# One weight step of the first MLP spread over two slots, on one core: bits in one, the two parts in the next

## The chip, the cores and the metric

The kernel runs on one core of a Trainium2 chip. The metric is device time in microseconds (us) of one execution; the medians below are over three runs. The core has five engines that work side by side and wait for each other through semaphores: TensorE (PE in the profile; its weight loads are the row PEld), VectorE (DVE), ScalarE (ACT), GpSimd (POOL) and SyncE (SP), the last two of which issue most transfers here.

## The reference

An attention with two kinds of masks over 4 sequences, and two MLPs behind it, all in float32 values; the weights come as float64.

```python
x = attention(q, k, v)                 # 8 heads, 576 positions, head size 64: (2304, 512)
h = x @ w_in                           # MLP 1, d_ff = 2048
g = h * clip(h + 3, 0, 6) / 6
x = g @ w_out
h = x @ w_in2                          # MLP 2
x = (max(h, 0) + log1p(exp(-abs(h)))) @ w_out2
```

Half of the heads see the last 32 positions ("local"), the other half every 32nd position ("strided").

## The kernel before, in words

Every float32 product is made of three products of a shorter type (fp32r): a value is split into its rounded part `hi` and the difference `lo`, and hi·hi, hi·lo and lo·hi are summed in PSUM. A weight needs more, since it comes as float64 words. `w_scale` (ACT, L132) scales its upper words, `w_bits` (DVE, L137 and L140) cuts the lower words and joins both to one float32 tile (`wir`, `wor`). After this, a split makes the two parts: `win_split` of a tile of w_in is a cast on ACT (`wih`, L160) and a difference on DVE (`wil`, L146, through the helper `less`); `wout_split` of a tile of w_out is the same with `woh` (L177) and `wol` (L146). The difference reads what the cast wrote.

MLP 1 runs over five chunks of tokens: chunk 0 has the first 96 positions of all four sequences (384 tokens), chunks 1 to 4 the other 480 of one sequence each. A chunk has 16 steps f, one for each 128 of d_ff. The program walks through `seq`, the 80 pairs (chunk, f), and calls `slot(n, ...)` for each; within a slot every engine keeps the order in which the program writes its instructions (`in_order`). Slot n does on TensorE the 12 matmuls of `pe_h(n)` (h, L774) and then the 12 of `pe_y(n-2)` (L818). Between them stand, for ACT and DVE, `post1` (ACT `r` L787, DVE `r` L788), `post2a` (ACT `gh` L795) and `post2b` (DVE `gl` L801), which make g and its two parts. PSUM has two banks for h, so pe_h(n) waits until DVE's `r` of slot n-2 has read its bank.

Chunk 0 is also the first use of each weight of MLP 1. So its slots carry the weights' work: `w_scale` and `win_bits` of w_in tile f+2, `win_split` of the same tile, and `w_scale`, `wout_bits`, `wout_split` of w_out tile f. `wout_split` also writes the float32 tile to `wdr` in DRAM (L176, issued by POOL), for chunk 1. The 32 loads of 512 KB (w_in L107, w_out L112) are issued by SP into eight buffers; `load_first(k)` issues the k-th of the list `order1`, and each waits until the tile that was in its buffer has been joined.

The attention of the sequence whose tokens come in the next chunk runs in between: `put(s, ...)` places a piece into half-slot s of the table `fill`, and slot n runs the pieces of half-slot 2n between pe_h and pe_y, and those of 2n+1 behind pe_y. For sequence 0 these are the transposes of q and k (`s_trans`), the scores (`a_qk`), mask, maximum, exponent and sum (`a_add`, `a_max`, `a_exp`, `a_sum`, `a_rec`), and the products with v (`a_pt`, `a_pv`, `a_px`), first for the strided heads, then for the local ones.

Of the kernel before, what the change touches and what calls it, by code (L numbers as in the profile page):

```python
# [7 lines left out]
F32 = mybir.dt.float32  # L8
F32R = mybir.dt.float32r
# [13 lines left out]
def attn_two_mlps(  # L23
# [21 lines left out]
    nc = tc.nc  # L45
# [6 lines left out]
    NF = DFF // P  # L52
# [36 lines left out]
    wdr = [dram.tile([P, DM], F32, name=f"wdr{f}") for f in range(NF)]  # L89
# [7 lines left out]
    wst_t, wi_t, wo_t = {}, {}, {}  # L97
# [14 lines left out]
        nc.sync.dma_start(out=t, in_=w_out[l][f * P : (f + 1) * P, :])  # L112
        wst_t[1, l, f] = t

    order1 = [(load_win, 0), (load_win, 1)]
    for f in range(NF):
        order1 += [(load_win, f + 2), (load_wout, f)]

    def load_first(k):
        load, f = order1[k] if k < len(order1) else (None, NF)  # L120
        if f < NF:
            load(0, f, k % 8)
# [6 lines left out]
    def w_scale(o, l, f):  # L129

        h = words(o, l, f, U32)[1].bitcast(F32)
        nc.scalar.activation(out=h, in_=h, func=AF.Prelu, scale=2.0**-112, alpha=-(2.0**32))  # L132

    def w_bits(o, l, f, out=None):
        low, _ = words(o, l, f, U32)
        m, e = words(o, l, f, I32)
        nc.vector.tensor_scalar(  # L137
            out=m, in0=low, scalar1=2.0**-29, scalar2=7.0, op0=ALU.mult, op1=ALU.min
        )
        nc.vector.scalar_tensor_tensor(  # L140
            out=e if out is None else out.bitcast(I32), in0=e, scalar=3, in1=m,
            op0=ALU.logical_shift_left, op1=ALU.bitwise_or,
        )
# [6 lines left out]
    def win_bits(f):  # L150
        wi_t[0, f] = sw_tile("wir", F32)
        w_bits(0, 0, f, wi_t[0, f])
        wst_t.pop((0, 0, f))

    def win_split(f):
        raw = wi_t[0, f]
        hi, lo = (wp.tile([P, KT, P], F32R, tag=f"wi{n}", name=f"wi{n}") for n in "hl")
        wi_t[0, f] = (hi, lo)
        hi, lo = (t.rearrange("p k f -> p (k f)") for t in (hi, lo))
        nc.scalar.copy(hi, raw)  # L160
        less(nc.vector, lo, raw, hi)

    def sw_tile(name, dt=F32R):
        return sw.tile([P, DM], dt, tag="sw", name=name)

    def wout_bits(f):
        wo_t[0, f] = tuple(
            sw_tile(n, dt) for n, dt in (("wor", F32), ("woh", F32R), ("wol", F32R))
        )
        w_bits(1, 0, f, wo_t[0, f][0])  # L170
        wst_t.pop((1, 0, f))

    def wout_split(f):
        raw, hi, lo = wo_t[0, f]
        wo_t[0, f] = hi, lo
        nc.gpsimd.dma_start(out=wdr[f], in_=raw)  # L176
        nc.scalar.copy(hi, raw)  # L177
        less(nc.vector, lo, raw, hi)

# [77 lines left out]
    def prep(k):  # L257

        n, h = divmod(k, 7)
        if k < 0 or n >= 2 * NF2:  # L260
            return
        o, g = divmod(n, NF2)
        if h == 0 and n + 1 < 2 * NF2:
            prep_load(*divmod(n + 1, NF2))
        if h < 2:
            w_scale(o, 1, 2 * g + h)
            w_bits(o, 1, 2 * g + h)
        elif h == 2:
            prep_sums(o, g)
        else:  # L270
            prep_split(o, g, *divmod(h - 3, 2))
# [511 lines left out]
    def post1(l, c, f):  # L783
        n = width(l, c)
        ps = ph_t.pop((l, c, f))[:, :n]
        r = tp.tile([P, SB], F32, tag="g32", name="r", bufs=2)[:, :n]
        nc.scalar.activation(out=r, in_=ps, func=AF.Relu, bias=3.0)  # L787
        mark["DVE"] = nc.vector.scalar_tensor_tensor(  # L788
            out=r, in0=r, scalar=6.0, in1=ps, op0=ALU.min, op1=ALU.mult
        )  # L790
        g32_t[l, c, f] = r

    def post2a(l, c, f):
        hi = gp.tile([P, SB], F32R, tag="gh", name="gh")[:, : width(l, c)]
        mark["ACT"] = nc.scalar.copy(hi, g32_t[l, c, f])  # L795
        g_t[l, c, f] = hi

    def post2b(l, c, f):
        hi = g_t[l, c, f]
        lo = gp.tile([P, SB], F32R, tag="gl", name="gl")[:, : width(l, c)]  # L800
        nc.vector.tensor_tensor(  # L801
            out=lo, in0=g32_t.pop((l, c, f)), in1=hi.bitcast(F32), op=ALU.subtract
        )
        g_t[l, c, f] = (hi, lo)
# [318 lines left out]
    def put(slot, u, *a):  # L1123
        fill.setdefault(max(slot, 0), []).append(lambda: u(*a))

    for b in range(B):
        o = 2 * NF * b
        s0 = o + 2 if b < 2 else o - 1
        for pr in range(NP):
            if b:  # L1130
                put(o - (14 if b > 1 else 5), s_load, b, pr)
                put(o - 5, s_load_v, b, pr)
            put(o + (6 if b < 2 else 3), l_load_qk, b, pr)
            put(o + 18, l_load_v, b, pr)
        if b == 0:
            for n, a in enumerate((("q",), ("k",), ("k", True))):
                put(s0 + n, s_trans, b, *a)
        else:
            for n, a in enumerate((n, pr) for pr in range(NP) for n in "qk"):
                put(s0 + n, s_trans32, b, *a)  # L1140
        for st, qk, pt in ((0, s0 + 4, 13), (1, o + 10, 22)):
            put(qk, a_qk, st, b)
            for e in range(2):
                put(qk + 1, a_add, st, b, e)
                put(qk + 2 + e, a_max, st, b, e)
                put(qk + 3 + e, a_exp, st, b, e)
                put(qk + 4 + e, a_sum, st, b, e)
            put(qk + 6, a_rec, st, b)
            put(o + pt, a_pt, st, b)
            put(o + pt + 3, a_pv, st, b)  # L1150
            put(o + pt + 6, a_px, st, b)

    with ExitStack():
# [5 lines left out]
        for i, t in enumerate(sq0):  # L1159
            nc.sync.dma_start(  # L1160
                out=t.rearrange("p (h i) d -> p h (i d)", h=2),
                in_=qs[:, 2 * i : 2 * i + 2, :II, :].rearrange("p h i d -> p h (i d)"),
# [15 lines left out]
            out=mask, in_=mask, compare_op=ALU.is_ge, fill=NEG / SCALE, base=STRIDE,  # L1178
# [85 lines left out]
        load_first(3)  # L1264
        bmask_make()
        load_first(4)
        for pr in range(NP):
            s_load(0, pr)
        for pr in range(NP):
            s_load_v(0, pr)  # L1270
        for k in range(5, 10):
            load_first(k)
        with after("xh", "xl"):
            win_split(1)

        seq = [(0, c, f) for c in range(NC1) for f in range(NF)]

        def slot(n, l, c, f):
            att = c < B
            first_use = c == 0  # L1280
            last1 = c == NC1 - 1
            k0 = 2 * n - 2 * NF - 14

            if n == NF + 1:
                prep_load(0, 0)
            if last1 and f == 0:
                at.close()
                l2p["x"] = ctx.enter_context(tc.tile_pool(name="l2x", bufs=1, reuse_waits="tile"))
            pe_h(l, c, f)
            if first_use:  # L1290
                if f + 2 < NF:
                    w_scale(0, 0, f + 2)
                    win_bits(f + 2)
            else:
                post1(l, c, f)
                post2a(l, c, f)
            if att:
                for u in fill.get(2 * n, []):
                    u()
            if first_use:  # L1300
                post1(l, c, f)
                post2a(l, c, f)
                if f + 2 < NF:
                    win_split(f + 2)
                w_scale(1, 0, f)
                wout_bits(f)
            post2b(l, c, f)
            prep(k0)
            if n >= 2:
                pe_y(*seq[n - 2])  # L1310
            if att:
                for u in fill.get(2 * n + 1, []):
                    u()
            prep(k0 + 1)
            if first_use:
                wout_split(f)
                load_first(2 * f + 10)
                load_first(2 * f + 11)
            if c == 1:
                split_raw(c, f)  # L1320
            if NF <= n + 3 < 2 * NF:
                load_raw(*seq[n + 3][1:])
            if 2 * NF <= n + 4 < len(seq):
                load_split(*seq[n + 4][1:])
            if last1 and f >= 1:
                kl, r = divmod(f - 1, 7)
                if r == 0 and kl < 2:
                    for o, i in x_load(CHS[0], kl):
                        nc.sync.dma_start(out=o, in_=i)
                elif r == 3:  # L1330
                    x_split(CHS[0], kl, 0)
                    x_sums(CHS[0], kl, False)
                elif r == 4:
                    x_sums(CHS[0], kl, True)
                    x_split(CHS[0], kl, 2)
                elif r == 5:
                    x_split(CHS[0], kl, 1)
# [149 lines left out]
```

## Time and profile before

| | us |
|---|---|
| median of 3 runs | 864.46 (863.44 to 866.81) |
| the profiled execution, its own time | 864.04 |
| its span, first to last instruction | 862.2 |

Busy share of the span: PE 96%, PEld 88%, DVE 74%, ACT 53%, POOL 10%. The mean granted clock of TensorE is 0.988 of full speed. The profile gives, for a stretch of the span, the busy time of each engine (x is the number of instructions), the granted clock and the load of the 16 DMA engines; for an engine, its instructions in order of time, with the time that it sat idle before one and the instruction that released it; and, for pairs of engines, the sum of such waits. A matmul's own duration is longer than the distance to the next one, since they overlap; the distance between two starts tells what one costs.

### The profile page before, as it was taken

What the parts mean: (1) busy time and instruction counts of PE and PEld (TensorE: products, weight loads), DVE (VectorE), ACT (ScalarE), POOL (GpSimd) and SP (SyncE); (2) the same over time, 40 slices, a digit from 0 to 9 for tenths busy, and PEclk for the clock granted to TensorE, in tenths of its full rate; (3) what the DMA queues carried; (4) which work ended last, traced back from release to release, by engine and by line L of the source; (5) the groups of instructions that cost most, each with busy time, mean ns of one, the idle gap of its engine ahead of it and who ended that gap; (6) DMA issues with size and microseconds to landing.
All of it is one profiled execution on the core that took longest, in us unless ns stands there. A gap on an engine that the chain in (4) does not pass through costs nothing.

```text
span 862.2 us, 16753 instructions
## 1 busy us (share of the span) xinstructions
PE 823.7 (96%) x6245; PEld 755.0 (88%) x6245; DVE 637.2 (74%) x1055; ACT 457.3 (53%) x754; POOL 88.4 (10%) x149
## 2 busy tenths in 40 slices
PE   4897899999999999999999999999999999999996
PEld 2796678888878888888888899999999999999995
DVE  5778777676767677866676848788678898587784
ACT  4555554455434445554555457863377844478530
POOL 3000003132311112111211110000000000000000
PEclk8899999999999999999999999999999999999999
DMA  8795888599987999696879599778899787997774
GB/s 244 216 323 163 230 189 303 174 230 350 352 337 227 247 331 318 210 278 212 304 257 319 197 348 298 244 247 249 247 308 343 241 247 224 301 300 242 252 245 110
DMA packets 169504, 225.42 MB, mean 261 GB/s; under 512 B 76432, under 2 KB 91664, under 8 KB 169424
## 3 DMA queue, kind: packets, MB, share of 16 engines
q1 hardware_dynamic: 154304, 176.71, 67.5%
q0 software_dynamic: 13312, 46.67, 14.2%
q10 hardware_dynamic: 1808, 0.98, 0.5%
q8 instruction: 50, 0.82, 0.4%
q14 instruction: 30, 0.25, 0.1%
HBM read 172.88 MB, written 51.38 MB: 260 GB/s over the span
## 4 chain that ended last, share of the span: by engine, by line
PE 54%; issue 16%; DVE 5%; ACT 4%; POOL 3%; DMA 2%; POOLq 0%; SPq 0%; DVEq 0%; ACTq 0%
PE psn L1075 15%; PE psm L931 11%; PE psy L818 10%; PE psh L774 10%; PE psa L1075 6%; POOL sdr L252 2%; DVE gq L913 2%; DVE gq L944 2%; ACT r L950 1%; DMA su<-sdr 1%; ACT r L979 1%; ACT r L949 1%; PE pso L715 1%; DVE u L913 1%; PE pss L639 1%
## 5 line engine op out<-in xcount | busy, mean ns | idle before, releaser
L931 PE MATMUL psm<-xh,su 128*128 128x384 f32 x672 | 172.1, 335 | 1.9 <-DVE u L913 1.8
L774 PE MATMUL psh<-xh,wih 128*128 128x480 f32 (+1 forms) x320 | 122.0, 381 | 4.0 <-ACT wih L160 2.8
L1075 PE MATMUL psn<-th,su 128*128 128x384 f32 x480 | 124.6, 339 | 0.0
L931 PEld LDWEIGHTS psm<-xh,su 128*128 128x128 f32 x672 | 121.5, 188 | 3.2 <-DVE u L913 3.2
L774 PE MATMUL psh<-xh,wil 128*128 128x480 f32 (+1 forms) x320 | 120.5, 377 | 0.7
L774 PE MATMUL psh<-xl,wih 128*128 128x480 f32 (+1 forms) x320 | 119.7, 374 | 1.2 <-issue 1.1
L818 PE MATMUL psy<-gh,woh 128*128 128x480 f32 (+1 forms) x320 | 120.1, 378 | 0.5 <-ACT gh L795 0.5
L818 PE MATMUL psy<-gh,wol 128*128 128x480 f32 (+1 forms) x320 | 119.8, 374 | 0.8 <-DVE wol L146 0.4
L818 PE MATMUL psy<-gl,woh 128*128 128x480 f32 (+1 forms) x320 | 118.7, 371 | 0.0
L931 PE MATMUL psm<-xl,su 128*128 128x384 f32 x336 | 112.3, 334 | 0.0
L1006 ACT CAST th<-gq 128x768 fp32r<-128x768 f32 x84 | 68.9, 834 | 69.7 <-PE psn L1075 43.0
L787 ACT ACTIVATE r<-psh 128x480 f32<-128x480 f32 (+1 forms) x80 | 44.4, 556 | 97.2 <-PE psh L774 97.0
L795 ACT CAST gh<-r 128x480 fp32r<-128x480 f32 (+1 forms) x80 | 46.2, 578 | 93.6 <-DVE r L788 93.6
L1075 PEld LDWEIGHTS psn<-th,su 128*128 128x128 f32 x480 | 87.5, 188 | 0.0
L788 DVE SCALAR_TENSOR_TENSOR r<-r,psh 128x480 f32<-128x480 f32 (+1 forms) x80 | 50.4, 630 | 46.2 <-ACT r L787 46.0
L1010 DVE TENSOR_TENSOR tl<-gq,th 128x768 fp32r<-128x768 f32 x84 | 77.7, 950 | 8.9 <-ACT th L1006 8.9
L1075 PE MATMUL psn<-tl,su 128*128 128x384 f32 x240 | 81.3, 339 | 0.0
L774 PEld LDWEIGHTS psh<-xh,wih 128*128 128x128 f32 x320 | 60.9, 190 | 13.7 <-ACT wih L160 4.7
L801 DVE TENSOR_TENSOR gl<-r,gh 128x480 fp32r<-128x480 f32 (+1 forms) x80 | 50.7, 633 | 26.2 <-ACT gh L795 26.0
L774 PEld LDWEIGHTS psh<-xh,wil 128*128 128x128 f32 x320 | 60.8, 190 | 10.1 <-DVE wil L146 2.6
L818 PEld LDWEIGHTS psy<-gh,wol 128*128 128x128 f32 x320 | 60.0, 188 | 10.6 <-DVE wol L146 2.4
L774 PEld LDWEIGHTS psh<-xl,wih 128*128 128x128 f32 x320 | 60.9, 190 | 9.4 <-issue 1.5
(143 smaller groups left out, 1400.6 us busy)
## 6 DMA issues: line engine op xcount, KB each, us to landing
su<-sdr SPq DMA_DIRECT2D x336, 256.0 KB
sdr<-so POOLq DMA_DIRECT2D x48, 512.0 KB, 4.9
wi<-in_w_in_dram SPq DMA_DIRECT2D x32, 512.0 KB
wo<-in_w_out_dram SPq DMA_DIRECT2D x32, 512.0 KB
woh<-wdh SPq DMA_DIRECT2D x48, 256.0 KB
wol<-wdl SPq DMA_DIRECT2D x48, 256.0 KB
wdr<-wor POOLq DMA_DIRECT2D x16, 256.0 KB, 4.6
wol<-wdr SPq DMA_DIRECT2D x16, 256.0 KB
```

What stands on the lines that cost most here:

```text
L252: nc.gpsimd.dma_start(out=sdr[o][g][4 * i + a : 4 * i + z].rearrange("b p n -> p b n"), in_=t.rearrange("p b j n -> p b (j n)").bitcast(F32),)
L774: mark["PE"] = nc.tensor.matmul(ps[:, :n], lhsT=w[:, kt], rhs=x[:, :n], start=(kt == 0 and j == 0), stop=(kt == KT - 1 and j == 2),)
L787: nc.scalar.activation(out=r, in_=ps, func=AF.Relu, bias=3.0)
L788: mark["DVE"] = nc.vector.scalar_tensor_tensor(out=r, in0=r, scalar=6.0, in1=ps, op0=ALU.min, op1=ALU.mult)
L795: mark["ACT"] = nc.scalar.copy(hi, g32_t[l, c, f])
L801: nc.vector.tensor_tensor(out=lo, in0=g32_t.pop((l, c, f)), in1=hi.bitcast(F32), op=ALU.subtract)
L818: mark["PE"] = nc.tensor.matmul(psy_t[l, c][m][:, :w], lhsT=a, rhs=bb, start=(f == 0 and j == 0), stop=(f == NF - 1 and j == 2),)
L913: return nc.vector.tensor_tensor(out=out_, in0=x, in1=y, op=op)
L931: nc.tensor.matmul(ps, lhsT=w[:, kl], rhs=x, start=i in (1, 5, 6) and kl == 0 and j == 0, stop=kl == 1 and j == 2, skip_group_check=True,)
L1006: nc.scalar.copy(tt[c, k][0], t_raw(c, k))
L1010: nc.vector.tensor_tensor(out=lo, in0=t_raw(c, k), in1=hi.bitcast(F32), op=ALU.subtract)
L1075: nc.tensor.matmul(psl[mt][:, :HT], lhsT=w[:, mt], rhs=x, start=i in (1, 4, 5, 6) and gg == 0 and j == 0, stop=gg == NF2 - 1 and j == 2, s ...
```

## The change

- `order1`: three tiles of w_in come before the first of w_out, so that each w_in tile is loaded one place earlier and each w_out tile one place later among the first few.
- At the start, tile 2 of w_in is scaled and joined before slot 0; slot f then scales and joins tile f+3, and splits tile f+2, which was joined a slot earlier.
- In slot f, the split of w_in tile f+2 stands ahead of `post1` (before: behind it), so that its ACT cast is issued before ACT's `r`, and its DVE difference before DVE's `r`.
- The attention's first half-slot of a slot comes behind `post1` in all chunks; before, chunk 0 had it ahead of `post1`, the other chunks behind `post2a`, where it stays.
- `wout_bits(f)` joins tile f of w_out and writes it to `wdr` at once; `post2a` (`gh`) comes behind it. The two parts are made by `wout_split(n-1)` in slot n, ahead of pe_y(n-2), so that w_out is split one slot after its bits.
- Sequence 0: transposes and scores of the strided heads, and the loads of the local q and k, stand a half-slot later (3 and 7 in place of 2 and 6).

```diff
-    order1 = [(load_win, 0), (load_win, 1)]
+    order1 = [(load_win, f) for f in range(3)]
     for f in range(NF):
-        order1 += [(load_win, f + 2), (load_wout, f)]
+        order1 += [(load_win, f + 3), (load_wout, f)]
...
     def wout_bits(f):
-        wo_t[0, f] = tuple(
-            sw_tile(n, dt) for n, dt in (("wor", F32), ("woh", F32R), ("wol", F32R))
-        )
-        w_bits(1, 0, f, wo_t[0, f][0])
+        raw = wo_t[0, f] = sw_tile("wor", F32)
+        w_bits(1, 0, f, raw)
         wst_t.pop((1, 0, f))
+        nc.gpsimd.dma_start(out=wdr[f], in_=raw)
 
     def wout_split(f):
-        raw, hi, lo = wo_t[0, f]
-        wo_t[0, f] = hi, lo
-        nc.gpsimd.dma_start(out=wdr[f], in_=raw)
+        raw = wo_t[0, f]
+        hi, lo = wo_t[0, f] = sw_tile("woh"), sw_tile("wol")
         nc.scalar.copy(hi, raw)
         less(nc.vector, lo, raw, hi)
...
-        s0 = o + 2 if b < 2 else o - 1
+        s0 = o + (3, 2, -1, -1)[b]
...
-            put(o + (6 if b < 2 else 3), l_load_qk, b, pr)
+            put(o + (7, 6, 3, 3)[b], l_load_qk, b, pr)
...
         with after("xh", "xl"):
             win_split(1)
+            w_scale(0, 0, 2)
+            win_bits(2)
...
             pe_h(l, c, f)
             if first_use:
+                if f + 3 < NF:
+                    w_scale(0, 0, f + 3)
+                    win_bits(f + 3)
                 if f + 2 < NF:
-                    w_scale(0, 0, f + 2)
-                    win_bits(f + 2)
-            else:
-                post1(l, c, f)
+                    win_split(f + 2)
+            post1(l, c, f)
+            if not first_use:
                 post2a(l, c, f)
             if att:
                 for u in fill.get(2 * n, []):
                     u()
             if first_use:
-                post1(l, c, f)
-                post2a(l, c, f)
-                if f + 2 < NF:
-                    win_split(f + 2)
                 w_scale(1, 0, f)
                 wout_bits(f)
+                post2a(l, c, f)
             post2b(l, c, f)
+            if 0 < n <= NF:
+                wout_split(n - 1)
...
             if first_use:
-                wout_split(f)
-                load_first(2 * f + 10)
                 load_first(2 * f + 11)
+                load_first(2 * f + 12)
```

DVE in slots 2 and 3 of chunk 0, before (`wi64` and `wo64` are the loaded words; the number behind a name tells the tiles apart):

```order
L788 SCALAR_TENSOR_TENSOR r_607<-r_607,psh_584 128x384
L146 TENSOR_TENSOR wil_613<-wir_598,wih_612 128x512
L137 TENSOR_SCALAR wo64_464<-wo64_464 128x512
L140 SCALAR_TENSOR_TENSOR wor_617<-wo64_464 128x512
L801 TENSOR_TENSOR gl_622<-r_607,gh_610 128x384
L146 TENSOR_TENSOR wol_619<-wor_617,woh_618 128x512
L137 TENSOR_SCALAR wi64_466<-wi64_466 128x512
L140 SCALAR_TENSOR_TENSOR wir_661<-wi64_466 128x512
L788 SCALAR_TENSOR_TENSOR r_740<-r_740,psh_647 128x384
```

And with the change, lines two lower:

```order
L786 SCALAR_TENSOR_TENSOR r_593<-r_593,psh_572 128x384
L137 TENSOR_SCALAR wo64_466<-wo64_466 128x512
L140 SCALAR_TENSOR_TENSOR wor_611<-wo64_466 128x512
L799 TENSOR_TENSOR gl_617<-r_593,gh_615 128x384
L146 TENSOR_TENSOR wol_620<-wor_542,woh_619 128x512
L137 TENSOR_SCALAR wi64_468<-wi64_468 128x512
L140 SCALAR_TENSOR_TENSOR wir_663<-wi64_468 128x512
L146 TENSOR_TENSOR wil_667<-wir_586,wih_666 128x512
L786 SCALAR_TENSOR_TENSOR r_670<-r_670,psh_649 128x384
```

The nine instructions of a slot are the same; `wil` has moved from right behind `r` to right ahead of the next `r`, and `wol` is now the difference of a tile (`wor_542`) joined in the slot before.

ACT from `r` of slot 3 to `r` of slot 4 of chunk 0, before:

```order
L787 ACTIVATE r_740<-psh_647 128x384
L795 CAST gh_743<-r_740 128x384
L160 CAST wih_745<-wir_661 128x512
L132 ACTIVATE wo64_468<-wo64_468 128x512
L177 CAST woh_751<-wor_750 128x512
L132 ACTIVATE wi64_511<-wi64_511 128x512
L787 ACTIVATE r_797<-psh_778 128x384
```

ACT in the same slots with the change:

```order
L785 ACTIVATE r_670<-psh_649 128x384
L132 ACTIVATE wo64_470<-wo64_470 128x512
L793 CAST gh_678<-r_670 128x384
L175 CAST woh_682<-wor_611 128x512
L132 ACTIVATE wi64_513<-wi64_513 128x512
L160 CAST wih_795<-wir_663 128x512
L785 ACTIVATE r_799<-psh_778 128x384
```

The cast `wih` stood behind `gh`, which reads DVE's `r`; now it stands behind the scaling of the next tile and ahead of the next `r`, and `woh` reads a `wor` of the slot before.

DVE at the start, from the last part of x for chunk 0 to the first `r`, with the change (before: `wil`, the first half of the bits of tile 2, `xl_214`, the second half, `r`):

```order
L283 TENSOR_TENSOR xl_218<-pst_393,xh_217 128x3x4x32
L137 TENSOR_SCALAR wi64_196<-wi64_196 128x512
L146 TENSOR_TENSOR wil_473<-wir_404,wih_472 128x512
L140 SCALAR_TENSOR_TENSOR wir_477<-wi64_196 128x512
L137 TENSOR_SCALAR wi64_407<-wi64_407 128x512
L283 TENSOR_TENSOR xl_214<-psd_380,xh_213 128x192
L140 SCALAR_TENSOR_TENSOR wir_494<-wi64_407 128x512
L146 TENSOR_TENSOR wil_498<-wir_477,wih_497 128x512
L786 SCALAR_TENSOR_TENSOR r_501<-r_501,psh_480 128x384
```

The last part of x (`xl_214`) now has two more instructions ahead of it. On ACT, likewise, two scalings (tiles 2 and 3) in place of one stand ahead of its `xh_213`. On SP, tiles 3 and 4 of w_in and tile 0 of w_out are now all loaded ahead of sequence 0's strided q, k and v, and tile 1 of w_out behind all of them; it stood ahead of the last two loads of v.

## Rows read from the trace of the kernel before

**Rows 1.** Busy time by stretch: before chunk 0, its slots, and all behind.
```profile
core 0: us, PE busy (x) PEld busy (x) DVE busy (x) ACT busy (x) POOL busy (x), PEclk, DMA share, GB/s
0.00:30.00 30.00, 17.01 (x119) 11.28 (x119) 19.53 (x54) 13.12 (x49) 7.60 (x17) 0.83 0.69 201
30.00:127.00 97.00, 83.23 (x918) 74.09 (x918) 75.17 (x142) 53.04 (x103) 7.76 (x14) 0.96 0.83 239
127.00:862.00 735.00, 723.49 (x5211) 669.58 (x5209) 542.49 (x861) 391.18 (x603) 73.02 (x118) 1.00 0.83 267
```

**Rows 2.** Waits from 30 to 127 us: who for whom, total us, times, longest.
```profile
DVE wil L146 <- ACT wih L160: 15.4, 14, 1.1
```

**Rows 3.** DVE in order of time: one slot without attention (start, duration, instruction, idle before).
```profile
40.13 0.69 DVE L146 TENSOR_TENSOR wil<-wir,wih 128x512 fp32r<-128x512 f32 x1 [1.10 <-ACT wih L160]
40.74 0.42 DVE L137 TENSOR_SCALAR wo<-wo 128x512 int32<-128x512 uint32 x1
41.26 0.69 DVE L140 SCALAR_TENSOR_TENSOR wor<-wo 128x512 int32<-128x512 int32 x1
41.87 0.55 DVE L801 TENSOR_TENSOR gl<-r,gh 128x384 fp32r<-128x384 f32 x1
42.64 0.69 DVE L146 TENSOR_TENSOR wol<-wor,woh 128x512 fp32r<-128x512 f32 x1 [0.22 <-ACT woh L177]
43.25 0.42 DVE L137 TENSOR_SCALAR wi<-wi 128x512 int32<-128x512 uint32 x1
43.78 0.69 DVE L140 SCALAR_TENSOR_TENSOR wir<-wi 128x512 int32<-128x512 int32 x1
44.38 0.55 DVE L788 SCALAR_TENSOR_TENSOR r<-r,psh 128x384 f32<-128x384 f32 x1
46.03 0.69 DVE L146 TENSOR_TENSOR wil<-wir,wih 128x512 fp32r<-128x512 f32 x1 [1.10 <-ACT wih L160]
```

**Rows 4.** DVE in order of time: the first `r` and the end of slot 9.
```profile
32.39 0.56 DVE L788 SCALAR_TENSOR_TENSOR r<-r,psh 128x384 f32<-128x384 f32 x1 [1.69 <-ACT r L787]
...
100.55 0.43 DVE L137 TENSOR_SCALAR wi<-wi 128x512 int32<-128x512 uint32 x1
```

**Rows 5.** PE in order of time: what pieces of chunk 0 cost, and chunk 1's first matmul.
```profile
108.54 1.48 PE L715 MATMUL pso<-vl,pt 64*32 64x64 f32 x128
109.95 0.44 PE L774 MATMUL psh<-xh,wih 128*128 128x384 f32 x1
...
112.16 0.34 PE L818 MATMUL psy<-gh,woh 128*128 128x384 f32 x1
...
118.93 1.09 PE L741 MATMUL psx<-ident,xn 128*128 128x128 f32 x8 [0.82 <-DVE xn L725]
119.78 0.42 PE L818 MATMUL psy<-gh,woh 128*128 128x384 f32 x1
...
127.26 0.38 PE L774 MATMUL psh<-xh,wih 128*128 128x480 f32 x1
```

**Rows 6.** DVE in order of time: the last part of x at the start.
```profile
29.76 0.35 DVE L285 TENSOR_TENSOR xl<-psd,xh 128x192 fp32r<-128x192 f32 x1
```

**Rows 7.** SP's queue: a weight load behind sequence 0's; busy time of the stretch around it.
```profile
31.94 0.93 SPq L107 DMA_DIRECT2D wi<-in_w_in_dram  x1
...
30.00:40.00 10.00, 7.08 (x43) 6.68 (x43) 5.73 (x11) 5.58 (x11) 0.72 (x1) 0.95 1.02 261
```

**Rows 8.** PE in order of time behind its longest wait of chunk 0.
```profile
69.35 1.62 PE L695 MATMUL psp<-ident,sc 128*128 128x128 f32 x8 [4.34 <-DVE sc L663]
...
71.09 0.52 PE L774 MATMUL psh<-xl,wih 128*128 128x384 f32 x1
71.41 0.52 PE L774 MATMUL psh<-xh,wil 128*128 128x384 f32 x1
```

**Rows 9.** Busy time by stretch: the later slots of chunk 0, and chunk 1 onwards.
```profile
80.00:127.00 47.00, 40.74 (x331) 33.58 (x330) 36.95 (x69) 25.33 (x48) 3.79 (x7) 1.00 0.84 208
...
127.00:300.00 173.00, 171.91 (x1789) 147.65 (x1788) 122.69 (x221) 81.82 (x149) 39.25 (x66) 1.00 0.87 274
```

More of the change, by code (lines that the diff above doesn't have):

```diff
@@ L1266, in attn_two_mlps @@
         load_first(4)
+        load_first(5)
         for pr in range(NP):
@@ L1270, in attn_two_mlps @@
             s_load_v(0, pr)
-        for k in range(5, 10):
+        for k in range(6, 11):
             load_first(k)
```

## The prediction

> **What bounds the kernel now.** I read the busy time by stretch first. Ahead of 30 us the first attention pieces are made; from 30 to 127 us run the slots of chunk 0; behind 127 us TensorE is busy for 723.5 of 735 us [rows 1]. So a microsecond gained behind 127 us would have to come out of the matmuls themselves, while chunk 0 leaves room: its 97 us hold 83.2 us of TensorE's busy time, and that is an overstatement, since a matmul's own duration overlaps the next one. Next, TensorE's instructions in order of time: the twelve matmuls of one pe_h take 112.16 - 109.95 = 2.2 us [rows 5], about 2.1 us without their start, and the twelve of pe_y the same. A slot without attention needs 4.3 us of TensorE. It gets 5.9 us: that is the distance between two `wil` of successive slots on DVE, 46.03 - 40.13 [rows 3].
>
> What DVE does in those 5.9 us is the point. It runs eight instructions back to back but for two waits, 1.10 us for the cast `wih` ahead of `wil` and 0.22 us for the cast `woh` ahead of `wol` [rows 3]. The sum of such waits says that the first is no accident: 14 times in chunk 0, never over 1.1 us, 15.4 us in all [rows 2]. It comes from the order: ACT's `wih` stands behind ACT's `gh`, `gh` needs DVE's `r`, and DVE has `wil` right behind that same `r`. So in every slot DVE sits through two ACT instructions. Without the two waits a slot costs DVE 5.90 - 1.10 - 0.22 = 4.6 us, just over TensorE's 4.3. DVE is the bound of most of chunk 0, TensorE is close behind it, and DVE's idle time there is time of the whole kernel.
>
> **The change, part by part.** I follow DVE from the first `r` to the end of slot 9, and TensorE from there to chunk 1's first matmul, since the last six slots have little attention work for DVE but several pieces for TensorE.
>
> *Waits on `wih` and `woh`.* In slots 0 to 9 DVE goes from 32.39 to 100.55, 68.2 us [rows 4]. Ten of the 14 waits lie there, 10 x 1.10 = 11.0 us, and four of the shorter ones, 4 x 0.22 = 0.9 us. In the new order `wih` stands ahead of ACT's `r`, on tiles joined a slot earlier, and `wil` has the two instructions of the bits ahead of it (1.14 us, 43.25 to 44.38 in [rows 3]); `woh` reads a tile of the slot before, and DVE has two bits and `gl` between `r` and `wol`. Both waits go. I take all 11.9 us; the other end is none of it, if ACT gets late elsewhere (below).
>
> *Work that changes its slot.* One `wil` now stands ahead of the first `r`, and slot 9 makes `wol` of tile 8 in place of 9: two differences of 0.61 us (43.25 - 42.64 [rows 3]) leave the stretch, 1.2 us. That is no gain by itself, since pe_y(8) needs only `wol` of tile 8, the last instruction of slot 9. The stretch becomes 68.2 - 11.9 - 1.2 = 55.1 us.
>
> *The start.* The last `xl` of chunk 0's x, without which pe_h(0) can't go on, has two more DVE instructions ahead of it, second half of the bits of tile 2 and first half of tile 3: 0.61 + 0.42 = 1.0 us by the like ones in [rows 3]. It started at 29.76 [rows 6] and TensorE takes it at once; the first `r`, which sat idle 1.69 us for ACT and so for pe_h(0) [rows 4], moves from 32.39 to 33.4. Bounds: 0.4 if `xl` slips through a gap, 1.6 with the extra scaling of 0.6 us or so on ACT.
>
> *Where TensorE is the later one.* In slots 2 and 3 TensorE has a group of transposes or scores on top, each between the 0.85 us of eight transposes (118.93 to 119.78) and the 1.41 us of 128 small matmuls (108.54 to 109.95) [rows 5], so 5.3 to 5.7 us against DVE's 4.6. Its lead is about a slot but has a limit: DVE needs pe_h(n) 1.75 us into its slot. I take 1.0 us of DVE waiting for TensorE, between 0 and 2. The half-slot by which sequence 0's transposes move decides only which slot pays this. From slot 4 on, DVE has its own attention work (mask, maximum, sums, each inside the 68.2 us), and TensorE follows it.
>
> *The end of chunk 0.* DVE ends slot 9 at 33.4 + 55.1 + 1.0 = 89.5. TensorE then has pe_y(8) to pe_y(13) and pe_h(11) to pe_h(15), 11 x 2.1 = 23.1 us, three attention groups of 0.85, 1.41 and 0.85 us, and some 0.4 us of starts between them: 26.6 us. DVE has 4.6 us a slot there and less from slot 13 on, where bits and `wil` of w_in run out, so TensorE is the bound and the last four `wih` waits are worth nothing. Chunk 1 begins at 116.1 in place of 127.26 [rows 5]: a gain of 11.2 us. Behind it TensorE is full as before, so the gain stays.
>
> *Loads.* A w_in tile is read a slot earlier and loaded a place earlier, so all but the first are where they were. The tight ones are tile 1 of w_out and tile 5 of w_in. The first load of w_in behind sequence 0's was issued at 31.94; around it 2.6 MB in 10 us moved [rows 7], which is four weight loads and the loads of v together. With one load more ahead and one less between, tile 1 of w_out is issued near 32.3 and, behind v and at that rate, in by about 36; DVE reads it near 37.9. Cost nothing; the cover is under 2 us, and a load later by more delays DVE by the excess. The write of `wdr` goes out a few instructions earlier, and POOL does nothing else there.
>
> *TensorE's clock.* Behind its longest wait, 4.34 us, TensorE ran at 1.2 GHz: starts 0.32 us apart, 71.09 to 71.41 [rows 8], for 0.175 at 2.4 GHz. From 80 to 127 us the granted clock is 1.00 [rows 9], though TensorE stops in nearly every slot for under 1.2 us. The forecast has no wait of TensorE over 2.5 us, and 12 slow matmuls would cost 1.7 us in a slot where it waits for DVE anyway; cost nothing. The Trainium skill, in "TensorE: Matmul & The Clock Gate", section on a second HAM failure mode, holds that short idle times between groups of matmuls make the clock swing between its levels; the rows of this kernel disagree, and what that would cost is the last rival.
>
> **Sum.** 864.04 of the profiled execution less 11.2 is **852.8 us**, 1.3% faster. Its own time is 0.4 us under the median of the runs, 864.46; a median of the changed kernel may stand as much above.
>
> **Rivals.**
>
> *The wait returns in another place.* ACT's `gh` now stands behind the scaling of w_out, `kT` copies and exponents stand between them in some slots, and DVE's `gl` and next `r` hang on ACT. Against: ACT is busy for 53.0 us in chunk 0 [rows 1], 3.3 us a slot, well under 4.6. If half a microsecond a slot came back in ten slots, 5 us, the time would be 858.
>
> *Transfers become the bound.* The DMA engines are at 0.83 for 97 us [rows 1], 80.5 us of work; in 86 us that is 0.94. For: from 30 to 40 us they are full [rows 7]. Against: the stretch right behind carries 274 GB/s at 0.87 while TensorE waits for nearly nothing [rows 9], and chunk 0 would want 239 x 97 / 86 = 270. If loads, or the DRAM copies that chunk 1 reads, pace the slots at today's rate, nearly all of the gain goes: 862.
>
> *It is all DVE.* If TensorE's lead covers its attention pieces, the late waits count too: the 15.4 us [rows 2] and the shorter ones, some 18 us less 1.0 for the start: 847.
>
> *Slower: TensorE falls to its lower clock.* If the stops that remain in every slot took the clock down as the 4.34 us did [rows 8], a slot's 24 matmuls would cost 24 x 0.145 = 3.5 us more. Slots 2 to 9 would take TensorE 8 x 7.7 + 7 us of attention, 69, where DVE needs about 48: 21 us more, 874. It decides from some four of the eight slots on: at four, 863. For: [rows 8]. Against: [rows 9], clock 1.00 with stops in every slot.
>
> That the change doesn't do what it says is excluded: the order of instructions on ACT and DVE is fixed within a slot, and shows the casts ahead of their differences.
>
> **Chances.** Forecast, 849 to 856: 0.66. Wait in another place, 856 to 860: 0.13. All DVE, 846 to 849: 0.08. Transfers, 860 to 864: 0.09. Lower clock: 0.04, about half of it within 0.5% and half above. Half a per cent, 4.3 us, is about what a measurement of this kernel can tell from no change. Faster by more than that holds the first three, 0.87; the same 0.11; slower 0.02. The range from 846 to 859 leaves out the last two rivals and a little at either end.
>
> **What would show it.** Right: DVE's waits for `wih` gone from chunk 0 or under 2 us in all; slots without attention 4.3 to 4.7 us apart; chunk 1's first matmul near 116 us; clock as before. The end of chunk 0 would show TensorE without waits from about slot 10. Wrong: DVE or ACT waiting for a transfer, ACT's `gh` waiting long behind a scaling with DVE idle at `gl`, `r` idle for ACT in most slots, or starts 0.32 us apart over many slots.

## The result, and the profile after

The changed kernel takes 854.32 us (median of 4 runs, 853.95 to 855.91), the kernel before 865.17 us beside it (4 runs, 863.44 to 866.81): 0.988 of the time, 95% interval 0.986 to 0.990. Forecast were 852.8 us and a range of 846 to 859. The profiled execution took 855.91 us, the longest of the four, with a span of 853.9 us. Lines stand two lower than before (`r` on DVE is L786, `gl` L799).

Busy time by stretch of the changed kernel (columns as in [rows 1]):

```profile
30.00:127.00 97.00, 89.51 (x965) 85.08 (x966) 80.85 (x155) 58.05 (x114) 9.93 (x18) 0.95 0.90 265
127.00:853.90 726.90, 715.46 (x5164) 662.75 (x5162) 535.32 (x848) 384.99 (x592) 70.73 (x114) 0.99 0.83 266
```

In the same 97 us TensorE starts 965 instructions where it started 918 [rows 1]: more of chunk 1 fits in. The rest shows where that came from. DVE in order of time, a slot without attention:

```profile
93.72 0.55 DVE L786 SCALAR_TENSOR_TENSOR r<-r,psh 128x384 f32<-128x384 f32 x1
94.19 0.42 DVE L137 TENSOR_SCALAR wo<-wo 128x512 int32<-128x512 uint32 x1
94.71 0.69 DVE L140 SCALAR_TENSOR_TENSOR wor<-wo 128x512 int32<-128x512 int32 x1
95.33 0.55 DVE L799 TENSOR_TENSOR gl<-r,gh 128x384 fp32r<-128x384 f32 x1
95.79 0.68 DVE L146 TENSOR_TENSOR wol<-wor,woh 128x512 fp32r<-128x512 f32 x1
96.39 0.42 DVE L137 TENSOR_SCALAR wi<-wi 128x512 int32<-128x512 uint32 x1
96.92 0.69 DVE L140 SCALAR_TENSOR_TENSOR wir<-wi 128x512 int32<-128x512 int32 x1
97.53 0.69 DVE L146 TENSOR_TENSOR wil<-wir,wih 128x512 fp32r<-128x512 f32 x1
98.13 0.55 DVE L786 SCALAR_TENSOR_TENSOR r<-r,psh 128x384 f32<-128x384 f32 x1
```

Eight instructions and no wait: 98.13 - 93.72 = 4.41 us for a slot that took 5.90 [rows 3]. The line of the 15.4 us for `wih` [rows 2] is gone from the waits. What stands there now, from 30 to 127 us (some lines: who for whom, total us, times, longest):

```profile
DVE r L786 <- ACT r L785: 9.4, 8, 2.0
...
PE psy L816 <- DVE wol L146: 3.9, 3, 2.2
...
PE psq L610 <- ACT qT L620: 3.1, 1, 3.1
ACT wo L132 <- DMA wo<-in_w_out_dram: 2.8, 1, 2.8
...
DVE wir L140 <- ACT wi L132: 1.7, 2, 1.3
...
DVE wo L137 <- DMA wo<-in_w_out_dram: 1.1, 1, 1.1
```

The first line is DVE waiting for TensorE: at the start, in slots 3 and 4, and from slot 13 on. The second is TensorE waiting for a difference that is made a slot later than before. The other four hang on one late load, and in part on the transposes that stand a half-slot later (e4 and e7 below). DVE's waits for loads and scalings in slots 0 to 9, with the first `r` and the end of slot 9:

```profile
33.24 0.56 DVE L786 SCALAR_TENSOR_TENSOR r<-r,psh 128x384 f32<-128x384 f32 x1 [1.08 <-ACT r L785]
...
38.67 0.43 DVE L137 TENSOR_SCALAR wo<-wo 128x512 int32<-128x512 uint32 x1 [1.07 <-DMA wo<-in_w_out_dram]
39.39 0.69 DVE L140 SCALAR_TENSOR_TENSOR wor<-wo 128x512 int32<-128x512 int32 x1 [0.29 <-ACT wo L132]
...
41.86 0.70 DVE L140 SCALAR_TENSOR_TENSOR wir<-wi 128x512 int32<-128x512 int32 x1 [0.37 <-ACT wi L132]
...
44.28 0.69 DVE L140 SCALAR_TENSOR_TENSOR wor<-wo 128x512 int32<-128x512 int32 x1 [0.32 <-ACT wo L132]
...
47.68 0.69 DVE L140 SCALAR_TENSOR_TENSOR wir<-wi 128x512 int32<-128x512 int32 x1 [1.29 <-ACT wi L132]
...
91.97 0.44 DVE L137 TENSOR_SCALAR wi<-wi 128x512 int32<-128x512 uint32 x1
```

SP's queue shows why tile 1 of w_out came late. In the kernel before it is issued between the four loads of v, which take 0.85 + 0.84 = 1.69 us; in the changed kernel behind all four, which take 3.30. The last of the three views shows what hung on it on ACT:

```profile
29.60 0.85 SPq L560 DMA_DIRECT2D vs<-in_vs_dram  x2
30.49 0.46 SPq L112 DMA_DIRECT2D wo<-in_w_out_dram  x1
31.05 0.84 SPq L560 DMA_DIRECT2D vs<-in_vs_dram  x2
```

```profile
30.37 3.30 SPq L558 DMA_DIRECT2D vs<-in_vs_dram  x4
33.72 0.66 SPq L112 DMA_DIRECT2D wo<-in_w_out_dram  x1
```

```profile
38.67 0.69 ACT L132 ACTIVATE wo<-wo 128x512 f32<-128x512 f32 x1 [2.84 <-DMA wo<-in_w_out_dram]
```

And TensorE waited for the copy `qT` that stood behind this scaling on ACT, and ran slowly from there (then the end of chunk 0: the start of pe_y(8) and chunk 1's first matmul):

```profile
40.81 1.94 PE L610 MATMUL psq<-ident,sk 126*128 126x126 f32 x8 [3.05 <-ACT qT L620]
...
43.19 0.52 PE L816 MATMUL psy<-gh,wol 128*128 128x384 f32 x1
43.51 0.52 PE L816 MATMUL psy<-gh,woh 128*128 128x384 f32 x1
...
90.59 0.34 PE L816 MATMUL psy<-gh,woh 128*128 128x384 f32 x1
...
118.04 0.38 PE L772 MATMUL psh<-xh,wih 128*128 128x480 f32 x1
```

```profile
40.00:50.00 10.00, 9.19 (x41) 9.10 (x42) 7.35 (x15) 7.45 (x17) 1.09 (x2) 0.66 1.03 413
```

Starts 0.32 us apart are the 1.2 GHz of [rows 8], and the granted clock of these 10 us is 0.66. The kernel before stops for the same copy and is slow behind it as well, but there DVE doesn't wait for it:

```profile
37.62 1.14 PE L612 MATMUL psq<-ident,sk 126*128 126x126 f32 x8 [2.81 <-ACT qT L622]
...
39.23 0.52 PE L774 MATMUL psh<-xh,wih 128*128 128x384 f32 x1
39.55 0.52 PE L774 MATMUL psh<-xl,wih 128*128 128x384 f32 x1
```

Chunk 1 begins at 118.04 in place of 127.26 [rows 5], 9.2 us sooner; from there to the end it is 853.9 - 118.04 = 735.9 us, before 862.2 - 127.26 = 734.9. This second number lies between 733.8 and 736.1 in all the kernels below, so the start of chunk 1's first matmul tells the time of an execution to within some 2 us.

### The profile page after: what moved, and what is told of

It reads as the page before. It is cut to its first block, busy times and chain, and to the rows that moved or that the text cites. A ratio compares the mean times of both kernels' runs of the same rounds, so it can differ in the third digit from the quotient of the medians.

```text
span 853.9 us, 16746 instructions
## 1 busy us (share of the span) xinstructions
PE 823.6 (96%) x6245; PEld 760.9 (89%) x6245; DVE 636.3 (75%) x1055; ACT 456.7 (53%) x754; POOL 88.3 (10%) x149
## 4 chain that ended last, share of the span: by engine, by line
PE 59%; issue 17%; DVE 9%; DMA 5%; ACT 4%; POOL 3%; SPq 2%; POOLq 0%; DVEq 0%; ACTq 0%
PE psn L1073 15%; PE psm L929 13%; PE psy L816 11%; PE psh L772 11%; PE psa L1073 6%; POOL sdr L250 2%; DVE gq L911 2%; DMA wo<-in_w_out_dram 2%; DVE gq L942 1%; DMA wi<-in_w_in_dram 1%; ACT r L948 1%; ACT r L977 1%; ACT r L947 1%; PE pso L713 1%; PE pss L637 1%
## 5 line engine op out<-in xcount | busy, mean ns | idle before, releaser
L786 DVE SCALAR_TENSOR_TENSOR r<-r,psh 128x480 f32<-128x480 f32 (+1 forms) x80 | 50.5, 631 | 52.8 <-ACT r L785 52.7
L799 DVE TENSOR_TENSOR gl<-r,gh 128x480 fp32r<-128x480 f32 (+1 forms) x80 | 50.6, 633 | 26.1 <-ACT gh L793 26.0
L816 PEld LDWEIGHTS psy<-gh,woh 128*128 128x128 f32 x320 | 60.6, 190 | 8.8 <-ACT gh L793 0.7
L250 POOL DMA_DIRECT2D sdr<-so x64 | 43.5, 681 | 239.5 <-DVE so L249 206.4
```

Source lines behind the costliest of these rows:

```text
L250: nc.gpsimd.dma_start(out=sdr[o][g][4 * i + a : 4 * i + z].rearrange("b p n -> p b n"), in_=t.rearrange("p b j n -> p b (j n)").bitcast(F32),)
L786: mark["DVE"] = nc.vector.scalar_tensor_tensor(out=r, in0=r, scalar=6.0, in1=ps, op0=ALU.min, op1=ALU.mult)
L799: nc.vector.tensor_tensor(out=lo, in0=g32_t.pop((l, c, f)), in1=hi.bitcast(F32), op=ALU.subtract)
L816: mark["PE"] = nc.tensor.matmul(psy_t[l, c][m][:, :w], lhsT=a, rhs=bb, start=(f == 0 and j == 0), stop=(f == NF - 1 and j == 2),)
```

## The experiments

Each is set against runs of the kernel before on the same chip (864.52 to 864.62 us, 11 to 23 runs); e1 to e4, e5 to e8 and e9 to e12 ran on three chips. The changed kernel's 854.32 us come from its own four runs above, so a difference of 1 or 2 us to them is not settled where the intervals of the ratios overlap. Each kernel has one traced execution, and what is read from traces holds for that one.

**The parts alone.** e1 has only the w_in half (tiles loaded one place earlier, bits in one slot, the two parts in the next, ahead of `r`):

```diff
 (before, slot f)
             pe_h(l, c, f)
             if first_use:
+                if f + 3 < NF:
+                    w_scale(0, 0, f + 3)
+                    win_bits(f + 3)
                 if f + 2 < NF:
-                    w_scale(0, 0, f + 2)
-                    win_bits(f + 2)
+                    win_split(f + 2)
...
                 post2a(l, c, f)
-                if f + 2 < NF:
-                    win_split(f + 2)
                 w_scale(1, 0, f)
                 wout_bits(f)
```

> Undoes the w_out half of the change: in chunk 0, tile f of w_out is joined and split in one slot as before; the w_in half (joined a slot ahead, split ahead of post1, loads in the new order) is kept, and sequence 0's attention stands where it stood. Theory (both halves are needed: a removed wait uncovers the next one): with w_in's difference gone from between DVE's r and the bits of w_out, DVE waits for ACT's scaling of w_out instead, as in slots 14 and 15 of before, 0.81 us (126.86 to 128.09), and 0.22 us for the cast of w_out stays; a slot gains only 0.3 us, 3 to 4 us in all: 860 to 862, ratio 0.996. Rival (each half is worth its own waits): ten times 1.10 us and the start as in the full change, 855 to 856.

Measured: 856.14 us (5 runs), ratio 0.990 (0.988 to 0.992). Most of the gain is here, and my theory fell. Its wait did appear, in the waits of e1 from 30 to 127 us:

```profile
DVE wor L140 <- ACT wo L132: 12.1, 15, 0.8
DVE wol L146 <- ACT woh L177: 2.0, 9, 0.3
```

But these 14.1 us in place of some 17 are not the whole bill. A recorded wait runs from the end of the instruction before; without a wait the next instruction starts 0.08 us ahead of that end (95.79 + 0.68 against 96.39, above). So every wait that goes is worth about 0.08 us more than its record; and where the waiting instruction itself takes 0.1 us to follow the bits (94.19 + 0.42 against 94.71), that much of the new wait is no loss. A slot without attention is 49.45 - 44.03 = 5.42 us by e1's `r`, 0.48 less than before; fifteen of them are 7.2 us. With 0.6 us for the later start (first `r` at 33.00) and 1.1 us for the bits of one tile that leave the last slots it is 7.7 us, and 127.26 - 119.66 = 7.6 us is what chunk 1 gained. That the two agree so well is partly luck: the sum counts DVE alone, and DVE's `r` of slot 14 comes 8.1 us sooner (118.31 for 126.40), so 0.5 us is lost behind it.

e2 has only the w_out half (bits and `wdr` in slot f, the parts in f+1), e3 only the half-slots of sequence 0:

```diff
 (e2, of before: with wout_bits and wout_split as in the change)
             post2b(l, c, f)
+            if 0 < n <= NF:
+                wout_split(n - 1)
...
-                wout_split(f)
 (e3, of before)
-        s0 = o + 2 if b < 2 else o - 1
+        s0 = o + (3, 2, -1, -1)[b]
-            put(o + (6 if b < 2 else 3), l_load_qk, b, pr)
+            put(o + (7, 6, 3, 3)[b], l_load_qk, b, pr)
```

> Undoes the w_in half: only w_out is split one slot after its bits and written to wdr at once; w_in, the loads and the attention stand as before. Theory: the wait of 1.10 us for the cast of w_in stays in every slot and only the 0.22 us behind it goes, and that in the slots without attention: 1 to 2 us, 863 to 864, ratio 0.998. Rival (the lag of w_out is what frees the engines): half of the gain or more, 859 or less.

> Only the half-slot of sequence 0's attention, in the kernel before. Theory: it decides only in which slot TensorE has these matmuls, and DVE is the bound: the same within 1 us, ratio 0.999 to 1.001. Rival (it relieves PSUM banks or the transfers of q and k at the start): 2 to 4 us faster.

Measured: e2 865.1 us (12 runs), ratio 1.001 (1.000 to 1.002); e3 864.9 us (12 runs), ratio 1.000 (0.999 to 1.002). Neither changes the time alone. e2's waits show a cost that I had not looked for:

```profile
PE psy L816 <- DVE wol L146: 7.7, 8, 1.2
PE psy L816 <- ACT woh L175: 4.4, 3, 1.9
```

In the kernel before, the first of these lines reads:

```profile
PE psy L818 <- DVE wol L146: 0.4, 1, 0.4
```

With the split a slot later, pe_y(n-2) of slot n reads what DVE makes last in slot n-1, so TensorE can't run further ahead of it. What that costs shows at the end of chunk 0: DVE starts `r` of slot 14 at 122.29 in e2, 4.1 us sooner than before (126.40), yet chunk 1's first matmul comes at 127.68, 0.4 us later than before. TensorE's lead, the distance by which it is ahead of DVE, has gone.

e4 is the changed kernel without the half-slots of e3:

> The changed kernel with sequence 0's attention where it stood before (transposes and scores at half-slots 2 and 6 in place of 3 and 7). Theory: in slot 1 ACT's copies of q then stand ahead of the scaling of w_out tile 1, which waits for its load, and not behind it; TensorE's wait of 3.05 us for them shrinks and with it the matmuls at 1.2 GHz behind it; 1 to 3 us faster than the changed kernel: 851 to 853. Rival (the later place is part of the gain): 1 to 2 us slower than the changed kernel, 855 to 856. If the place matters for nothing: 854.3 within 0.7.

Measured: 852.17 us (4 runs), ratio 0.985 (0.982 to 0.987), 2.2 us below the changed kernel. The time is in the theory's range, but its interval overlaps the changed kernel's 0.986 to 0.990, so the time alone doesn't settle it. The trace is as expected, with TensorE's stop for `qT` at 0.70 us, no slow matmuls from 30 to 80 us, and the end of slot 9 on DVE at 88.07 in place of 91.97. DVE still waits 1.02 us for tile 1 of w_out there; the wait of 1.29 us for a scaling, and those of `r` in slots 3 and 4, are gone.

**Who is the bound where.** e5 makes each `wol` of slots 4 to 9 twice, e6 each of slots 10 to 15; both write the same values again:

```diff
         less(nc.vector, lo, raw, hi)
+        if 3 <= f < 9:          (e6: 9 <= f < 15)
+            less(nc.vector, lo, raw, hi)
```

> The changed kernel with the difference of w_out made twice in slots 4 to 9 (0.61 us more DVE each, 3.7 us in all). Theory (DVE is the bound up to slot 9): the time rises by all or nearly all of it, 3 to 4 us, to 857.3 to 858.3. Rival (TensorE is the bound throughout, DVE only follows): within 1 us of the changed kernel.

> The same doubling in slots 10 to 15, again 3.7 us more DVE. Theory (TensorE is the bound from slot 10 on): 0 to 1.2 us more than the changed kernel, since DVE idles over 5 us for it in slots 13 to 16; 854.3 to 855.5. Rival (DVE is the bound to the end of chunk 0): 3 to 4 us more, 857 to 858.

Measured: e5 858.39 us (6 runs), ratio 0.993 (0.991 to 0.995), 4.1 us over the changed kernel. The work added is more than the 3.7 us expected: a doubled `wol` takes DVE 1.33 us in e5's trace (63.78 to 65.11), 0.72 more than one, so six add 4.3. e6 854.64 us (5 runs), ratio 0.988 (0.986 to 0.990), 0.3 us over it. `r` of slot 4, slot 9's end on DVE and chunk 1's first matmul, e5 and then e6:

```profile
54.13 0.55 DVE L788 SCALAR_TENSOR_TENSOR r<-r,psh 128x384 f32<-128x384 f32 x1 [1.44 <-ACT r L787]
...
95.15 0.48 DVE L137 TENSOR_SCALAR wi<-wi 128x512 int32<-128x512 uint32 x1
...
121.33 0.38 PE L774 MATMUL psh<-xh,wih 128*128 128x480 f32 x1
```

```profile
52.59 0.56 DVE L788 SCALAR_TENSOR_TENSOR r<-r,psh 128x384 f32<-128x384 f32 x1 [1.40 <-ACT r L787]
...
89.26 0.43 DVE L137 TENSOR_SCALAR wi<-wi 128x512 int32<-128x512 uint32 x1
...
116.84 0.38 PE L774 MATMUL psh<-xh,wih 128*128 128x480 f32 x1
```

From `r` of slot 4 to slot 9's end e5 takes 95.15 - 54.13 = 41.0 us and e6, without the added work there, 89.26 - 52.59 = 36.7: all of the 4.3 us show. From slot 9's end to chunk 1 it takes e5 26.2 us and e6, with 4.3 us more for DVE in that stretch, 27.6; the changed kernel takes 26.1. So DVE is the bound up to slot 9, as the prediction split the sum, and TensorE mostly behind it: 1.5 of 4.3 us show there. (Slot 9 ends sooner in e6's execution than in that of the changed kernel, though both run the same program up to there: tile 1 of w_out was issued at 31.33, not at 33.72, DVE waits for no load, and TensorE's stop for `qT` is 1.4 us, not 3.1. So the late load differs between executions.)

**The late load and the start.** e7 issues the weight loads ahead of sequence 0's v; e8 puts the bits of w_in tiles 2 and 3 behind the last part of x:

```diff
 (e7, of the changed kernel)
+        for k in range(6, 11):
+            load_first(k)
         for pr in range(NP):
             s_load_v(0, pr)
-        for k in range(6, 11):
-            load_first(k)
 (e8, of the changed kernel; xeh and xel mark the last part of x)
             win_split(1)
+        with after("xeh", "xel"):
             w_scale(0, 0, 2)
             win_bits(2)
```

> The changed kernel with sequence 0's four loads of v behind the next five weight loads, so that tile 1 of w_out is issued some 3 us earlier. Theory (its load, which DVE waited for 1.07 us and ACT for 2.84, starts a chain: q copied late, TensorE waits 3.05 us, a dozen matmuls at 1.2 GHz, then r and the scalings late in slots 2 to 4): 2.5 to 4 us faster, 850.5 to 852. Rival (only the 1.07 us that DVE itself waited): 1 us, 853.3. Rival (TensorE's stop is due to its own order and the load is hidden): no change.

> The changed kernel with the scalings and bits of tiles 2 and 3 of w_in ordered behind the last part of chunk 0's x, at the start. Theory: pe_h(0) goes on about 1.4 us earlier, the first r about 0.6 us, since its own bits now stand ahead of it: 0.5 to 1 us faster, 853.3 to 853.8, if the load of tile 1 of w_out doesn't hold slot 1 at the same time as before; if it does, no change. Rival (the start sets everything behind it): 1.4 us faster, 852.9.

Measured: e7 852.75 us (4 runs), ratio 0.986 (0.985 to 0.988), 1.6 us below the changed kernel, between the two; its interval, too, overlaps that of the changed kernel. DVE waits for no transfer there, TensorE 0.2 us for `qT`, and slot 9 ends at 89.60. e8 855.24 us (4 runs), ratio 0.989 (0.988 to 0.991): no gain, as expected where the load holds slot 1 (TensorE still stops 3.8 us for `qT`). e7 has a price: the loads of v behind the weights take SP far longer, and what SP issues next is late.

```profile
32.03 7.37 SPq L558 DMA_DIRECT2D vs<-in_vs_dram  x4
```

e9 joins e4 and e7, e10 adds e8's edit to that:

> Changed kernel with attention of sequence 0 at its old half-steps (as in e4) and the weight loads issued ahead of sequence 0's v (as in e7). Theory that both heal the same delay (TensorE's stop at the transposes of slot 1, caused by the late tile of w_out): together little more than the better one, 851.3 to 852.3 us. Rival, that they heal different ones (-2.2 and -1.6 us add up): 850 to 851. Chunk 1's first matmul would start at 114 to 115 us by the first, at 112.5 to 113.5 by the second.

> e9 with the bits of w_in tiles 2 and 3 behind the last part of x, as in e8. With no load holding slot 1, the 1.0 us that the prediction charged to the start should come back: first r at 32.3 to 32.6, time 0.5 to 1.0 us below e9. Rival: the bits are only moved behind x and are needed in slot 0 and 1 anyway, so r of slot 1 stands where it stood: within 0.3 us of e9.

Measured: e9 852.75 us (6 runs, 849.3 to 857.09), ratio 0.986 (0.984 to 0.989); e10 852.03 us (4 runs), ratio 0.985 (0.983 to 0.987). Joined, the two are no better than either, so the gains don't add; e9 is above even the first theory's 852.3, and in the traced execution, the second longest of the six, chunk 1 begins at 117.59, not at 114 to 115. SP spends 8.1 us on v there, and TensorE stops for the local k:

```profile
57.79 1.17 PE L637 MATMUL pss<-lk,lq 64*32 64x64 f32 x64 [2.51 <-DMA lk<-in_kl_dram]
```

DVE's `r` of slot 6 then waits 2.91 us. e10's first `r` starts at 31.54, sooner than forecast, but its `r` of slot 6 waits 4.29 us for TensorE, which stopped at the same scores (3.54 and 1.16 us). Its intervals and e9's overlap, so whether the start is worth anything isn't settled.

**Work off DVE.** e11 is e9 with `wol` of slots 4 to 9 on GpSimd:

```diff
-        less(nc.vector, lo, raw, hi)
+        less(nc.gpsimd if 3 <= f < 9 else nc.vector, lo, raw, hi)
```

> e9 with the difference wol of slots 4 to 9 on GpSimd in place of VectorE. VectorE has 6 x 0.61 = 3.7 us less in the slots in which e5 showed it as the bound. Theory: TensorE, whose slot of 4.3 us and attention pieces stand close behind, takes over: 1 to 2 us below e9, with waits of VectorE's r for ScalarE's r from slot 5 or 6 on in place of slot 13. Rival 1: all 3.7 us. Rival 2: VectorE and GpSimd slow each other down when both stream (VectorE's 128x512 instructions longer than 0.69 us) or GpSimd's difference comes too late for pe_y: no gain or a loss of up to 2 us.

Measured: 852.77 us (5 runs), ratio 0.986 (0.984 to 0.989): nothing gained, rival 2; DVE waits for TensorE from slot 13 on, as in the changed kernel, not from slot 5 or 6. GpSimd's difference, and DVE's instruction that began beside it:

```profile
54.24 1.27 POOL L146 TENSOR_TENSOR wol<-wor,woh 128x512 fp32r<-128x512 f32 x1
```

```profile
54.26 1.58 DVE L671 TENSOR_TENSOR sc<-sc,nm 128x288 f32<-128x288 f32 x1
```

This `sc` takes 0.46 us elsewhere. Four of the six differences have such a case beside them (1.58, 1.62, 1.60 and 1.91 us for 0.46, 0.69, 0.42 and 0.69); they cost DVE 4.5 us where six differences saved it 3.7. TensorE also waited 4.1 us for GpSimd's `wol`. The Trainium skill, "SBUF — State Buffer", section on who interferes with whom, has VectorE instructions with two SBUF inputs, or in a two-port mode, blocked and not slowed by a GpSimd instruction that reads SBUF; these durations, about one GpSimd instruction longer, agree in size, though in two of the four cases the profile has DVE's instruction start first, by 0.02 and 0.07 us.

**One line in place of the w_out half.** e12 is e1 with ACT's scaling of the w_out tile ahead of `gh`:

```diff
                 post1(l, c, f)
-                post2a(l, c, f)
                 w_scale(1, 0, f)
+                post2a(l, c, f)
                 wout_bits(f)
```

> e1 (the w_in half alone) with ScalarE's scaling of the w_out tile ahead of gh in place of behind it. Theory: the 12.1 us that VectorE's wor waits for that scaling in e1 are what e1 lacks beside the changed kernel; they go, and as VectorE then is 0.7 us a slot faster until TensorE is the bound: 852.5 to 854.3 us. Rival: TensorE is the bound of e1 already, its chunk 1 starts only 1.6 us behind that of the changed kernel: 855.5 to 856.5, and VectorE waits in another place.

Measured: 848.15 us (4 runs, 847.6 to 849.35), ratio 0.981 (0.980 to 0.982). That is 8.0 us below e1, 6.2 below the changed kernel's median, and below the theory's range: the best kernel here. Its interval touches only that of e4, at its end, and single runs of e4, e9 and e10 come as low as 848.9 to 849.3. Its slots are not shorter than the changed kernel's: 48.36 - 43.64 = 4.72 us by `r`, since `wol` waits 0.22 us for `woh`. Of the 6.4 us by which its chunk 1 begins sooner than the changed kernel's, 2.2 are there when DVE ends slot 9; the other 4.1 lie in TensorE's place. The start of pe_y(9), slot 9's end on DVE, and chunk 1's first matmul in e12:

```profile
89.69 0.42 PE L818 MATMUL psy<-gh,woh 128*128 128x384 f32 x1
...
111.68 0.38 PE L774 MATMUL psh<-xh,wih 128*128 128x480 f32 x1
```

```profile
89.73 0.43 DVE L137 TENSOR_SCALAR wi<-wi 128x512 int32<-128x512 uint32 x1
```

When DVE ends slot 9, TensorE of e12 begins pe_y(9); that of the changed kernel is in pe_y(8), which began at 90.59, and comes to pe_y(9) only at 95.57, 3.6 us later: the rest of pe_y(8), pe_h(11) and eight transposes stand between. The work behind is the same, but the changed kernel takes 0.5 us more for it, 0.36 of them a wait for `wol`. So 111.68 - 89.73 = 22.0 us remain in place of 26.1. Here `wol` of tile f is made in slot f and read two slots later, and TensorE waits for it nowhere in chunk 0. e4, the nearest kernel with the split a slot later, waits for it 2.7 us and needs 114.97 - 88.07 = 26.9 us. e4 and e12 also differ in where the attention's first half-slot stands (behind `post1` or ahead of it), and no run separates that.

## Why the prediction was right, and where it was off

*Waits on `wih` and `woh`.* Right: both are gone, 11.9 us were counted. They were worth more: a slot without attention is 4.41 us, forecast 4.6, since each wait cost some 0.08 us above its record. Ten waits for `wih` and four for `woh` make that 1.1 us.

*The start.* Right: the first `r` at 33.24, forecast 33.4.

*Where TensorE is the later one.* 1.0 us was taken, between 0 and 2; `r` of slots 3 and 4 waited 0.68 and 1.16 us, 1.8 together, behind the slow matmuls. That the half-slot of sequence 0 only decides which slot pays doesn't hold in the traces: in e4, without it, `r` waits in none of the slots 1 to 12. How much of e4's 2.2 us this is stays open; the load was issued 0.8 us sooner in its execution.

*Loads.* This is the step that failed. "Cost nothing; the cover is under 2 us" took the issue of tile 1 of w_out at 32.3 and its arrival at about 36. SP needed 3.30 us for the four loads of v, where they had taken 1.69, so the tile was issued at 33.72; it was there at 38.67, and DVE had been ready for it 1.07 us before. With the wait for it go those for scalings, 1.07 + 0.29 + 0.37 + 0.32 + 1.29 = 3.3 us in all, the longest of them only together with the later half-slot, as e4 shows. With these, the stretch comes out nearly as it was: 55.1 - 1.1 + 3.3 + 1.8 = 59.1 us, and 91.97 - 33.24 = 58.7 was measured. The size belongs to this execution, the longest of the four: e4 and e7, in which the chain is cut, begin chunk 1 at 114.97 and 115.64, 2.4 to 3.1 us sooner.

*TensorE's clock.* "The forecast has no wait of TensorE over 2.5 us" failed: 3.05 us, and pe_y(0) at 1.2 GHz, 12 x 0.32 = 3.8 us for 2.1. The trace before had a warning that I passed over, its stop of 2.81 us for the same copy with 1.2 GHz behind it; there it cost nothing, as in e3, whose stop of 4.1 us leaves the time as it was. A stop of 2.20 us in a later slot of the changed kernel was followed by starts 0.32 us apart, too. The lower-clock rival stayed away nonetheless: from 80 to 127 us the granted clock is 1.00, as in [rows 9], with two stops of 1.31 and 0.36 us.

*The end of chunk 0.* Right: 26.1 us from slot 9's end, forecast 26.6, and DVE waits for TensorE's `r` from slot 13 on. e5 and e6 confirm the border.

*The sum.* Chunk 1 at 118.04, forecast 116.1: +1.9; behind it 735.9 us for 734.9: +1.0. 852.8 + 2.9 = 855.7, the profiled execution's 855.91. The other three runs stand at 854.0 to 854.4. That the forecast comes so near owes something to luck: the stretch up to slot 9 took 2.6 us more than forecast, it would have been 3.7 had the waits been worth only their records, and the start and the end of chunk 0 gave 0.7 back.

*Rivals.* The wait in another place is what e1 does (0.80 to 0.84 us at `wor` in every slot); the changed kernel doesn't. The DMA engines, at 0.90 for 97 us, don't set the pace: in e12, the fastest, they are at 0.99 from 80 to 127 us. "All DVE" is excluded by e6, in which some two thirds of DVE's added work costs nothing.

What the prediction didn't see is the price of the w_out half. I wrote that pe_y(8) needs only `wol` of tile 8, DVE's last instruction of slot 9, and counted it neither as gain nor as loss. It costs TensorE some of its lead, 3.6 us at the end of slot 9 beside e12, as the traces of e2 and e12 suggest, and it stands in the 26.6 us that I took for given. No run changes the place of `wol` alone in the changed kernel, so the size isn't shown by itself.

## What to carry to other kernels

Order a producer's two steps so that the second engine never waits for the first within the same slot, but look at the consumer too: a product made a slot later takes from the consumer's lead, and the lead is what pays for its extra work later. Try the smallest reordering first; here, one line moved on ACT, on top of the w_in half, was worth 8.0 us, where the w_out half and the half-slots together were worth 1.8. A wait can be worth a little more than its record (0.08 us here), since an instruction that isn't held starts ahead of the end of the one before.

## What the hardware showed that I had not expected

- SP's time to issue the same four loads of v differs with what stands ahead of them: 1.69 us before, 3.30 in the changed kernel, 7.4 and 8.1 us behind four weight loads (e7, e9). What SP issues next is late with it. What in the queue makes it so, no run separates.
- A GpSimd difference of 1.27 us stretched a DVE instruction beside it by 0.9 to 1.2 us in four of six cases (e11), so work given to GpSimd came back on DVE.
- Executions of one kernel differ by several us: e9's six runs go from 849.3 to 857.09 us, e12's four from 847.6 to 849.35. The early load can be one reason (issued at 33.72 in the changed kernel's execution, at 31.33 in e6's, with the same program up to there); since one execution of each is traced, it isn't shown to be all of it.
